# A Strassen step inside the fifth product of the last gate and up stage, with its weight sums kept in DRAM

## The chip, the cores and the metric

The kernel runs on one core of a Trainium2 chip. The metric is device time in microseconds (us) of one execution, lower is better, given as the median of several executions. TensorE (PE) multiplies, VectorE (DVE), ScalarE (ACT) and GpSimd (POOL) work element by element, and SyncE (SP) issues most of the transfers (DMAs).

## The reference

Four residual layers over x of 2048 tokens by 1024 features. Layers 0 and 2 are linear attention (A) with 32 heads, layers 1 and 3 a gated unit (B) of width 3584.

```python
def _A_ref(x, wqkv, wo):                    # phi(t) = (t + 1 if t > 0 else exp(t)) + 1e-6
    q, k, v = split_heads(x @ wqkv)
    kv = einsum("bhsd,bhse->bhde", phi(k), v);  z = phi(k).sum(tokens)
    return merge_heads((phi(q) @ kv) / (phi(q) @ z + 1e-6)) @ wo

def _B_ref(x, W_gate, W_up, W_down):
    gate, up = x @ W_gate, x @ W_up         # (2048 x 1024) @ (1024 x 3584)
    return (relu(gate) * up) @ W_down

x = A_x
x = x + _A_ref(layernorm(x), A_wqkv, A_wo)
x = x + _B_ref(layernorm(x), W_gate, W_up, W_down)
x = x + _A_ref(layernorm(x), A_wqkv, A_wo)
x = x + _B_ref(layernorm(x), W_gate, W_up, W_down)
```

## The kernel before

Each large product is done by the Strassen-Winograd scheme: two matrices of 2x2 blocks are multiplied with seven block products in place of eight, from sums of blocks of the activations and of the weights. In layer B the tokens are worked on in two chunks `c` of 1024, and the columns of gate and up in 14 units `u` of 256 each. `glu` (the function with the matmul line L1154) does one unit: seven products for gate (`g`) and seven for up (`u`), each of four 128x128 weight tiles by 512 token columns, accumulated in one bank of PSUM (the accumulator memory). So a unit is 56 matmuls. The products are numbered as in the text: `five` uses the activation sum s1 (a21 + a22) and is copied by ACT from its bank to a tile `m5` (L1171); `one` goes to bank x, which ACT copies to bank y (L1177); `two` adds to x, `six` adds to y; DVE adds m5 to y, which gives z (L1190); `seven` adds to y and DVE adds the result to m5 (L1203); `three` adds to z, `four` to y. The relus `r` of gate (L1162) and the products `h` (L1165, `put`; L1207 on POOL) close each of the four output blocks. The order of a unit is: five g, one g, five u, one u, two g, six g, two u, six u, 7 g, 3 g, 7 u, 3 u, 4 g, 4 u. A matmul line in the profile names the bank that it writes, so `yg` is product one's bank after six, seven or four, and `vg` is product five.

Where each sum of blocks stands:

- Sums of activations: `sums_x` (L1127 to L1130), four DVE operations for each of four column blocks, ahead of the chunk that uses them.
- Sums of gate and up weights: `make_gu` (L1064 to L1067), made once, in layer 1 chunk 0, by DVE for the unit that comes next, and stored in DRAM as `tg` and `tu` by DMAs on ACT's queue (L1068), one for each weight. All later chunks load the raw weights and these sums again through a ring of buffers (`load_gu`, SP's queue), whose loads are issued five entries ahead of use.
- Sums of down weights: `sums_d`, and for some products of the down stage a second level, `make_dd` and `sums_dd` (L1038), with results in DRAM (`dd`). Those products ("deep", L1319) run seven inner products of 256 columns.

The order of the side work is set by `later`: `later.at(n, f)` runs `f` after n further products (turns), since `mm` in `glu` calls `later.tick()`. `behind(op, f)` issues the operations of f after op on their engine. Instructions of an engine run in the order of issue, and DMAs of SP's queue are issued in SP's order, where one that waits holds back those behind it.

In layer A at the start of layer 2, `phi` (L435, L436, L439) makes the feature map: two ACT operations (relu, exp) into a tile e and one DVE operation. The layer norm of a further group of tokens runs beside it: DVE statistics and `mv` (L195), `ln_root` (ACT, L173 and L174) and the scaled slab (DVE, L180), which a transposing DMA on SP turns to xnT (L410). Query products are the groups qx, qv, qy, qz (L677), with sums by ACT (L670) and DVE (L699, L703).

Of the kernel before, what the change touches and what calls it, by code (L numbers as in the profile page):

```python
# [14 lines left out]
P = 128  # L15
# [77 lines left out]
class _Net:  # L93
    def __init__(self, tc, ctx, x_d, wqkv_d, wo_d, wg_d, wu_d, wd_d, out_d):
# [35 lines left out]
        self.tw = {n: self.spill.tile([P, 8, NW], F16, name=f"t{n}") for n in ("q0", "q1", "k0", "k1")}  # L130
        self.dd = {p: self.spill.tile([P, 7, self.U // 2, NW // 2], F16, name=f"dd{p}") for p in self.DEEP}
        self.later = _Later()
        self.phi_lag = 0
# [50 lines left out]
    def ln_norm(self, layer, t):  # L184
# [14 lines left out]
        def scale(rstd=None if layer == 2 else rstd):  # L199
            if rstd is None:  # L200
                rstd = self.ln_root(mv)
                return lambda: scale(rstd)
# [228 lines left out]
    def phi(self, ps, out):  # L431

        nc = self.nc
        e = self.temp()
        nc.scalar.activation(out=e, in_=ps, func=ACT.Relu, scale=-1.0)  # L435
        nc.scalar.activation(out=e, in_=e, func=ACT.Exp, scale=-1.0, bias=self.eps6[:, 0:1])  # L436

        def join():
            self.last_phi = nc.vector.scalar_tensor_tensor(out=out, in0=ps, scalar=1e-6, in1=e,  # L439
                                                           op0=ALU.max, op1=ALU.add)  # L440

        if self.phi_lag:
            self.later.at(self.phi_lag, join)
        else:
            join()
# [524 lines left out]
    def plan_B(self, l):  # L970
        for c in range(2):
            for u in range(self.U):
                for w in "gu":
                    self.ring.add((l, c, w, u), lambda t, w=w, u=u, first=(l == 1 and c == 0):
                                  self.load_gu(t, w, u, first))
            for p in self.order_d(l, c):
# [64 lines left out]
    def make_dd(self, p, at):  # L1041

        self.later.at(at, lambda: self.load_dd(p))
        for n in range(4):
            self.later.at(at + 18 + 4 * n, lambda n=n: self.behind(self.last_put, lambda n: self.sums_dd(p, n), (n,)))

    def raw_gu(self, t):
        return t[:, 0:4, :].rearrange("p a (b f) -> p (a b) f", f=2 * P)
# [3 lines left out]

    def load_gu(self, t, w, u, first):
        self.nc.sync.dma_start(out=self.raw_gu(t),
                               in_=self.wgu_v[w][:, :, u * 2 * P:(u + 1) * 2 * P])
        if not first:
            self.nc.sync.dma_start(out=t[:, 4:8, :].bitcast(F16), in_=self.tgu[w, u])

# [73 lines left out]
    def ln_chunk(self, l, c, first, step, lag, after):  # L1132
        for j in range(QT):
            for h in range(2):
                self.ln_at(first + (2 * j + h) * step, l, (2 * c + h) * QT + j, lag, after)
            self.later.at(39 + 3 * j, lambda j=j: self.behind(
                self.last_on, lambda j: self.sums_x(l, c, j), (j,)))

    def glu(self, l, c, u, hT):

# [11 lines left out]
        def mm(w, m, ps, start=False):  # L1152
            for k in range(4):
                nc.tensor.matmul(ps, lhsT=W[w][m][:, k, :], rhs=A[m][:, k, :],  # L1154
                                 start=start and k == 0, stop=k == 3, skip_group_check=True)
            later.tick()

        h = hT[u // 2][:, (u % 2) * 4:(u % 2) * 4 + 4, :]
        V, X, Y, Z, R = {}, {}, {}, {}, {}
# [32 lines left out]
        if c == 0 and u == 0:  # L1192
            for f in (one, two, five, six):
                for w in "gu":
                    f(w)
        else:
            for f, f2 in ((five, one), (two, six)):
# [243 lines left out]
    def layer_B(self, l, final):  # L1441
# [6 lines left out]
        for c in range(2):  # L1448
# [3 lines left out]
            for u in range(self.U):  # L1452
# [3 lines left out]
                if first:  # L1456
                    if u + 1 < self.U:
                        self.later.at(4 if u else 9, lambda u=u: behind(self.last_put if u else self.last_z, lambda: [
                            self.make_gu(ring.get((l, c, w, u + 1)), w, u + 1) for w in "gu"]))
                    if u == 3:  # L1460
# [9 lines left out]
                if not final and c == 1:  # L1470
                    if u in (0, 3):
                        self.load_w("qk"[u // 3])
                    if u in (1, 2, 4, 5):
                        for n in range(2):
                            self.later.at(4 + 5 * n, lambda w="qk"[u // 4], n=2 * (u % 3 - 1) + n: behind(
                                self.last_put, lambda: self.sums_w(w, n)))
                if (l, c, u) in ((1, 1, 6), (3, 0, 4)):
                    self.make_dd("T4" if l == 1 else "21", 1)
# [76 lines left out]
```

## Time and profile before

| quantity | value |
|---|---|
| median of three runs | 1448.4 us (1448.38 to 1448.63) |
| the profiled execution | 1447.77 us |
| its span, first to last instruction | 1446.0 us |
| granted TensorE clock | 1.000 |
| busy: PE, DVE, ACT, POOL | 1437.7, 959.7, 613.8, 309.6 us |
| matmuls | 7430 |
| DMA traffic | 304.90 MB |

A time in us from the span's start tells the stage. Layer 1 chunk 0 runs its gate and up products from about 207 to 397; layer 2 starts at 736; layer 3 chunk 0 has gate and up from about 937 to 1113 and the last chunk from about 1194 to 1363, with its down stage up to the end. In a row of the timeline the columns are start, duration, engine, line, operation, output and input; the bracket says how long the engine had been idle and which instruction ended the wait. In a row by stage each engine's busy time is followed by its instruction count in brackets, and the last three columns are granted clock, share of DMA time and GB/s. A row of the chain holds start, length, engine, line and number of instructions. Matmuls overlap, so a group of four appears 1.03 us long in the timeline, though groups start closer together.

### The profile page before, as it was taken

The numbers are of one execution on the slowest core, as the hardware profiler recorded it, in microseconds if no ns is written. First come the engines' busy times: TensorE is split into PE (matmuls) and PEld (weight loads), VectorE is DVE, ScalarE is ACT, GpSimd is POOL, SyncE is SP. The second block draws the span as 40 slices with busy tenths as digits, with TensorE's granted clock in tenths as the row PEclk, the third lists the DMA queues.
The fourth block names the chain that finished last, engine by engine and source line by source line (L and its number), as shares of the span: only waits on it lengthen the run. The fifth ranks groups of instructions, "written<-read, shape, count | busy, mean of one in ns | idle before, by whom it ended". The sixth has DMA issues, their size and how long they took to land.

```text
span 1446.0 us, 20268 instructions
## 1 busy us (share of the span) xinstructions
PE 1437.7 (99%) x7430; PEld 709.2 (49%) x7430; DVE 959.7 (66%) x1799; ACT 613.8 (42%) x1113; POOL 309.6 (21%) x221
## 2 busy tenths in 40 slices
PE   9999999999999999999999999999999999999998
PEld 4444444444455444445654444444444574444457
DVE  7978698677594456549687885764445864444595
ACT  7872564233334334332168726633333433333300
POOL 1453861011100011110031586410111011111002
PEclk9999999999999999999999999999999999999999
DMA  9950787997469999646973119968644799444465
GB/s 287 237 161 8 176 212 204 288 333 255 162 213 288 355 307 307 202 127 220 297 253 88 58 30 266 261 233 269 217 146 130 220 293 323 146 146 146 153 234 181
DMA packets 328836, 304.90 MB, mean 211 GB/s; under 512 B 107456, under 2 KB 291776, under 8 KB 327712
## 3 DMA queue, kind: packets, MB, share of 16 engines
q1 hardware_dynamic: 320688, 282.30, 65.8%
q10 hardware_dynamic: 6560, 17.24, 3.1%
q0 software_dynamic: 1488, 4.07, 0.8%
q8 instruction: 58, 0.95, 0.3%
q14 instruction: 42, 0.34, 0.1%
HBM read 227.28 MB, written 51.64 MB: 193 GB/s over the span
## 4 chain that ended last, share of the span: by engine, by line
PE 92%; DVE 5%; ACT 1%; issue 1%; DMA 1%; SPq 0%; DVEq 0%; ACTq 0%
PE yu L1154 10%; PE yg L1154 10%; PE ps L493 10%; PE dy L1267 8%; PE xu L1154 6%; PE xg L1154 6%; PE dx L1267 6%; PE ps L776 4%; PE zu L1154 3%; PE vg L1154 3%; PE vu L1154 3%; PE zg L1154 3%; PE my L575 3%; PE dyT L1319 2%; PE mv L575 2%; PE mx L575 2%
## 5 line engine op out<-in xcount | busy, mean ns | idle before, releaser
L1154 PEld LDWEIGHTS <-w 128*128 128x128 f16 (+1 forms) x3136 | 306.7, 98 | 372.4 <-issue 3.6
L1207 POOL TENSOR_TENSOR h<-m5u,m5g 128x512 f16<-128x512 f32 x56 | 72.7, 1298 | 721.1 <-DVE m5u L1203 660.0
L493 PE MATMUL ps<-w,xnT 128*128 128x512 bf16 x768 | 169.9, 379 | 0.5 <-ACT xnT L348 0.3
L1190 DVE TENSOR_TENSOR zg<-yg,m5g 128x512 f32<-128x512 f32 x56 | 39.1, 699 | 180.2 <-PE yg L1154 176.1
L493 PEld LDWEIGHTS <-xnT 128*128 128x128 bf16 x768 | 74.4, 98 | 90.0 <-issue 1.6
L1154 PE MATMUL yg<-s,w 128*128 128x512 f16 x448 | 115.0, 379 | 0.3 <-DVE zg L1190 0.3
L1154 PE MATMUL yu<-s,w 128*128 128x512 f16 x448 | 114.9, 379 | 0.1
L1154 PE MATMUL xu<-xnT,w 128*128 128x512 f16 x448 | 115.0, 379 | 0.0
L1154 PE MATMUL xg<-xnT,w 128*128 128x512 f16 x448 | 115.0, 379 | 0.0
L1267 PEld LDWEIGHTS <-h 128*128 128x128 f16 x672 | 65.7, 98 | 78.3
L1162 ACT ACTIVATE m5g<-m5g 128x512 f32<-128x512 f32 x56 | 35.2, 628 | 155.0 <-DVE m5g L1203 155.0
L1319 PEld LDWEIGHTS <-h 128*128 128x128 f16 x966 | 94.5, 98 | 12.3
L436 ACT ACTIVATE e<-e,eps 128x512 f32<-128x512 f32 x128 | 91.0, 720 | 3.2
L723 POOL TENSOR_TENSOR kvc<-pq,kvc 128x1024 f32<-128x1024 bf16 x32 | 78.5, 2454 | 53.1 <-DVE den L728 32.8
L1267 PE MATMUL dx<-w,h 128*128 128x512 bf16 x392 | 85.3, 379 | 0.0
L776 PE MATMUL ps<-T,pqT 128*128 128x512 bf16 x384 | 83.6, 379 | 0.0
L1171 ACT ACTIVATE m5g<-vg 128x512 f32<-128x512 f32 x56 | 33.4, 597 | 108.5 <-PE vg L1154 108.5
L1165 DVE TENSOR_TENSOR h<-yu,r 128x512 f16<-128x512 f32 x56 | 38.7, 691 | 52.8 <-PE yu L1154 52.8
L514 POOL TENSOR_TENSOR kvc<-kvc,slab 128x512 f32<-128x512 f32 x46 | 57.2, 1249 | 76.0 <-DVE slab L439 72.7
L1162 ACT ACTIVATE r<-yg 128x512 f32<-128x512 f32 x56 | 33.4, 597 | 85.2 <-PE yg L1154 85.2
L1203 DVE TENSOR_TENSOR m5u<-yu,m5u 128x512 f32<-128x512 f32 x56 | 38.7, 690 | 46.3 <-PE yu L1154 46.3
L435 ACT ACTIVATE e<-ps 128x512 f32<-128x512 f32 x92 | 54.2, 589 | 28.9 <-PE ps L493 28.8
(234 smaller groups left out, 2385.5 us busy)
## 6 DMA issues: line engine op xcount, KB each, us to landing
w<-in_B_W_gate_dram SPq DMA_DIRECT2D x56, 512.0 KB, 6.1
w<-in_B_W_up_dram SPq DMA_DIRECT2D x56, 512.0 KB, 6.0
w<-tg SPq DMA_DIRECT2D x42, 512.0 KB, 7.3
w<-tu SPq DMA_DIRECT2D x42, 512.0 KB, 6.6
w<-ddT SPq DMA_DIRECT2D x21, 896.0 KB, 6.5
w<-td SPq DMA_DIRECT2D x18, 896.0 KB, 5.0
w<-dd SPq DMA_DIRECT2D x15, 896.0 KB, 5.0
w<-in_B_W_down_dram SPq DMA_DIRECT2D x14, 896.0 KB, 4.9
```

The source lines that it names most:

```text
L435: nc.scalar.activation(out=e, in_=ps, func=ACT.Relu, scale=-1.0)
L436: nc.scalar.activation(out=e, in_=e, func=ACT.Exp, scale=-1.0, bias=self.eps6[:, 0:1])
L493: nc.tensor.matmul(by_row(ps), lhsT=self.xnT[l, l_q][:, kt, j * P:(j + 1) * P], rhs=w[:, kt, :].rearrange("p (b i d) -> p i b d", i=R, d=H ...
L514: nc.gpsimd.tensor_tensor(out=ksum[:, cols], in0=ksum[:, cols], in1=pk, op=ALU.add)
L575: nc.tensor.matmul(banks[j], lhsT=A(i)[:, j * P:(j + 1) * P], rhs=B(i), start=start and i == 0, stop=i == NS - 1, skip_group_check=True)
L723: nc.gpsimd.tensor_tensor(out=prod, in0=pq_of[sc, j], in1=zrow, op=ALU.mult)
L776: nc.tensor.matmul(ps, lhsT=pqT[sc][:, g, j * P:(j + 1) * P], rhs=T[g // 4][:, g % 4, n2 * NW:(n2 + 1) * NW], start=(g == 0), stop=(g == G ...
L1154: nc.tensor.matmul(ps, lhsT=W[w][m][:, k, :], rhs=A[m][:, k, :], start=start and k == 0, stop=k == 3, skip_group_check=True)
L1162: self.last_relu = nc.scalar.activation(out=out, in_=ps, func=ACT.Relu)
L1207: nc.gpsimd.tensor_tensor(out=h[:, 3, :], in0=V["u"], in1=V["g"], op=ALU.mult)
L1267: nc.tensor.matmul(banks[j], lhsT=A(k)[:, j * P:(j + 1) * P], rhs=w[:, i, :], start=start and k == 0, stop=k == self.U - 1, skip_group_che ...
L1319: nc.tensor.matmul(bank[:, j * H:(j + 1) * H], lhsT=A[i // 2][:, i % 2, j * P:(j + 1) * P], rhs=B[m][:, i, :], start=start and i == 0 and ...
```

## The change

In layer 3 chunk 1, product five of gate and up of two neighbouring units (an even u from 2 on, and u + 1) is done together, as a 2x2 block product of its own in seven inner products: `inner_gi` returns them in the order five, one, two, six, seven, three, four, each of four matmuls of 256 columns (weight tiles of gate or up, both halves). They are put in after turns 0, 2, 3, 5, 7, 9 and 11 of the odd unit before the pair; the results go to two SBUF tiles `gi_v`, used in turns by the pairs. The units 2 to 13 leave out their own product five and start one g, one u, two g, six g, two u, six u; the rest is as before. `ready_gi` makes the four inner activation sums once, in unit 0.

The inner weights are 7 sets: three are blocks of the sum for product five that lie in `tg` and `tu` already, and four are differences. `make_gi` runs in layer 3 chunk 0 at units 3, 7 and 9, for two pairs each: it loads the four blocks (8 DMAs), stores three of them as they are, and has DVE make four more (`sums`, eight DVE operations for two pairs) with a store behind each. `load_gi` reads all seven sets of a pair in one DMA of SP at the start of an even unit, into one buffer `gi_w` that lies over two tiles of the residual x. `load_gu` leaves out that quarter of the sums from unit 2 of the last chunk on.

Besides, at layer 2's start `ln_root` is issued behind the last exponential of the feature map (`last_exp`). And in layer 1 chunk 0 `make_gu` for the next unit no longer runs for gate and up at one turn (turn 4, or 9 for unit 0): gate stays there and up follows four turns later.

```diff
--- before.py
+++ after.py
@@ -129,6 +129,7 @@
         self.td = self.spill.tile([P, 4, self.U, NW], F16, name="td")
         self.tw = {n: self.spill.tile([P, 8, NW], F16, name=f"t{n}") for n in ("q0", "q1", "k0", "k1")}
         self.dd = {p: self.spill.tile([P, 7, self.U // 2, NW // 2], F16, name=f"dd{p}") for p in self.DEEP}
+        self.gi = [self.spill.tile([P, 7, 2, 2, P], F16, name=f"gi{p}") for p in range(self.U // 2)]
         self.later = _Later()
         self.phi_lag = 0
 
@@ -198,7 +199,8 @@
 
         def scale(rstd=None if layer == 2 else rstd):
             if rstd is None:
-                rstd = self.ln_root(mv)
+                with self.tc.issue_after(self.last_exp.ins):
+                    rstd = self.ln_root(mv)
                 return lambda: scale(rstd)
             if layer % 2 == 0 and (layer, t // QT) != (2, 0):
                 return self.ln_scale(src, mv, rstd, self.xn_home(layer, t))
@@ -433,7 +435,7 @@
         nc = self.nc
         e = self.temp()
         nc.scalar.activation(out=e, in_=ps, func=ACT.Relu, scale=-1.0)
-        nc.scalar.activation(out=e, in_=e, func=ACT.Exp, scale=-1.0, bias=self.eps6[:, 0:1])
+        self.last_exp = nc.scalar.activation(out=e, in_=e, func=ACT.Exp, scale=-1.0, bias=self.eps6[:, 0:1])
 
         def join():
             self.last_phi = nc.vector.scalar_tensor_tensor(out=out, in0=ps, scalar=1e-6, in1=e,
@@ -971,8 +973,8 @@
         for c in range(2):
             for u in range(self.U):
                 for w in "gu":
-                    self.ring.add((l, c, w, u), lambda t, w=w, u=u, first=(l == 1 and c == 0):
-                                  self.load_gu(t, w, u, first))
+                    self.ring.add((l, c, w, u), lambda t, w=w, u=u, first=(l == 1 and c == 0),
+                                  lo=(l, c) == (3, 1) and u > 1: self.load_gu(t, w, u, first, lo))
             for p in self.order_d(l, c):
                 if self.is_deep(l, c, p):
                     for e in range(4):
@@ -1044,17 +1046,118 @@
         for n in range(4):
             self.later.at(at + 18 + 4 * n, lambda n=n: self.behind(self.last_put, lambda n: self.sums_dd(p, n), (n,)))
 
+    GI_AT = (0, 3, 5), (1, 4, 2, 6)
+
+    def make_gi(self, pairs, at):
+
+        def load():
+            t = self.slot(f"gi{pairs[0]}", [P, 2, 2, 2, 4, P], F16)
+            for i, p in enumerate(pairs):
+                for a in range(2):
+                    for n, w in enumerate("gu"):
+                        self.nc.sync.dma_start(out=t[:, i, n, a, :, :].rearrange("p k f -> p (k f)"),
+                                               in_=self.tgu[w, 2 * p + a][:, 0, :])
+            self.gi_b = [[[t[:, i, :, a, 2 * j:2 * j + 2, :] for a in range(2)] for j in range(2)]
+                         for i in range(2)]
+            self.later.at(4, lambda: [store(i, m, self.gi_b[i][j][a]) for i in range(2)
+                                      for m, j, a in ((0, 0, 0), (3, 1, 0), (5, 1, 1))])
+
+        def store(i, m, b):
+            for n in range(2):
+                self.nc.sync.dma_start(out=self.gi[pairs[i]][:, m, n, :, :], in_=b[:, n, :, :])
+
+        def sums(i, n):
+            (b11, b12), (b21, b22) = self.gi_b[i]
+            out, a, b, m = ((b11, b12, b11, 1), (b12, b22, b12, 4), (b22, b22, b11, 2), (b21, b21, b22, 6))[n]
+            self.nc.vector.tensor_tensor(out=out, in0=a, in1=b, op=ALU.subtract)
+            self.later.at(2, lambda: store(i, m, out))
+
+        self.later.at(at, load)
+        for i in range(2):
+            for n in range(4):
+                self.later.at(at + 12 + 2 * (4 * i + n), lambda i=i, n=n: self.behind(
+                    self.last_put, lambda n: sums(i, n), (n,)))
+
+    def inner_gi(self, p):
+
+        nc, v = self.nc, self.nc.vector
+        H, V, A = NW // 2, self.gi_v[p % 2], self.gi_a
+        B = {m: self.gi_w[:, n] for n, m in enumerate((1, 5, 6, 2, 7, 3, 4))}
+        out = lambda i, a: V[:, a, :, i, :]
+        copy = lambda o, x: nc.scalar.activation(out=o, in_=x, func=ACT.Copy)
+        bank = lambda k: self.kvp.tile([P, 2, H], F32, tag=f"kv{k}", name=f"i{k}")
+        S = {}
+
+        def mm(m, b, start=False):
+            for w in range(2):
+                for k in range(2):
+                    nc.tensor.matmul(b[:, w, :], lhsT=B[m][:, w, k, :], rhs=A[m][:, k, :],
+                                     start=start and w == 0 and k == 0, stop=k == 1, skip_group_check=True)
+
+        def five():
+            z = bank(0)
+            mm(5, z, True)
+            copy(out(1, 1), z)
+
+        def one():
+            S["x"], S["y"] = bank(0), bank(1)
+            mm(1, S["x"], True)
+            copy(S["y"], S["x"])
+
+        def two():
+            mm(2, S["x"])
+            copy(out(0, 0), S["x"])
+
+        def six():
+            mm(6, S["y"])
+            S["z"] = bank(0)
+            v.tensor_tensor(out=S["z"], in0=S["y"], in1=out(1, 1), op=ALU.add)
+
+        def seven():
+            mm(7, S["y"])
+            v.tensor_tensor(out=out(1, 1), in0=S["y"], in1=out(1, 1), op=ALU.add)
+
+        def three():
+            mm(3, S["z"])
+            copy(out(0, 1), S["z"])
+
+        def four():
+            mm(4, S["y"])
+            copy(out(1, 0), S["y"])
+
+        return [five, one, two, six, seven, three, four]
+
+    def ready_gi(self):
+
+        flat = lambda t: self.xall[:, t:t + 2, :].rearrange("p a n -> p (a n)")
+        H = NW // 2
+        self.gi_w = flat(0).bitcast(F16)[:, 0:28 * P].rearrange("p (m w k f) -> p m w k f", m=7, w=2, f=P)
+        self.gi_v = [flat(t).rearrange("p (a w i n) -> p a w i n", a=2, w=2, n=H) for t in (2, 4)]
+        S1, S2, S3, S4 = (self.x[6].bitcast(F16)[:, n * NW:(n + 1) * NW].rearrange("p (k n) -> p k n", n=H)
+                          for n in range(4))
+        s1 = self.xs[3, 1][0]
+        (a11, a12), (a21, a22) = ([s1[:, 2 * j:2 * j + 2, i * H:(i + 1) * H] for j in range(2)] for i in range(2))
+        v = self.nc.vector
+        v.tensor_tensor(out=S1, in0=a21, in1=a22, op=ALU.add)
+        v.tensor_tensor(out=S2, in0=S1, in1=a11, op=ALU.subtract)
+        v.tensor_tensor(out=S3, in0=a11, in1=a21, op=ALU.subtract)
+        v.tensor_tensor(out=S4, in0=a12, in1=S2, op=ALU.subtract)
+        self.gi_a = {1: a11, 2: a12, 3: S4, 4: a22, 5: S1, 6: S2, 7: S3}
+
+    def load_gi(self, p):
+        self.nc.sync.dma_start(out=self.gi_w, in_=self.gi[p])
+
     def raw_gu(self, t):
         return t[:, 0:4, :].rearrange("p a (b f) -> p (a b) f", f=2 * P)
 
     def sums_gu(self, t):
         return t[:, 4:8, :].bitcast(F16).rearrange("p t (k f) -> p t k f", f=P)
 
-    def load_gu(self, t, w, u, first):
+    def load_gu(self, t, w, u, first, lo):
         self.nc.sync.dma_start(out=self.raw_gu(t),
                                in_=self.wgu_v[w][:, :, u * 2 * P:(u + 1) * 2 * P])
         if not first:
-            self.nc.sync.dma_start(out=t[:, 4:8, :].bitcast(F16), in_=self.tgu[w, u])
+            self.nc.sync.dma_start(out=t[:, 4 + lo:8, :].bitcast(F16), in_=self.tgu[w, u][:, lo:4, :])
 
     def make_gu(self, t, w, u):
 
@@ -1136,6 +1239,8 @@
             self.later.at(39 + 3 * j, lambda j=j: self.behind(
                 self.last_on, lambda j: self.sums_x(l, c, j), (j,)))
 
+    INNER_AT = (0, 2, 3, 5, 7, 9, 11)
+
     def glu(self, l, c, u, hT):
 
         nc, later = self.nc, self.later
@@ -1153,8 +1258,13 @@
             for k in range(4):
                 nc.tensor.matmul(ps, lhsT=W[w][m][:, k, :], rhs=A[m][:, k, :],
                                  start=start and k == 0, stop=k == 3, skip_group_check=True)
+            if inner and next(turn) in self.INNER_AT:
+                inner.pop(0)()
             later.tick()
 
+        deep = (l, c) == (3, 1)
+        inner = self.inner_gi(u // 2 + 1) if deep and u % 2 and u + 1 < self.U else []
+        turn = count(0 if u > 1 else -2)
         h = hT[u // 2][:, (u % 2) * 4:(u % 2) * 4 + 4, :]
         V, X, Y, Z, R = {}, {}, {}, {}, {}
 
@@ -1193,6 +1303,13 @@
             for f in (one, two, five, six):
                 for w in "gu":
                     f(w)
+        elif deep and u > 1:
+            for k, w in enumerate("gu"):
+                V[w] = self.gi_v[u // 2 % 2][:, u % 2, k, :, :].rearrange("p i n -> p (i n)")
+            for f in ((one,), (two, six)):
+                for w in "gu":
+                    for g in f:
+                        g(w)
         else:
             for f, f2 in ((five, one), (two, six)):
                 for w in "gu":
@@ -1455,8 +1572,10 @@
                 ring.load_to(ring.index((l, c, "g", u)) + 5)
                 if first:
                     if u + 1 < self.U:
-                        self.later.at(4 if u else 9, lambda u=u: behind(self.last_put if u else self.last_z, lambda: [
-                            self.make_gu(ring.get((l, c, w, u + 1)), w, u + 1) for w in "gu"]))
+                        for n, w in enumerate("gu"):
+                            self.later.at((4 if u else 9) + 4 * n, lambda u=u, w=w: behind(
+                                self.last_put if u else self.last_z,
+                                lambda: self.make_gu(ring.get((l, c, w, u + 1)), w, u + 1)))
                     if u == 3:
                         for d in (self.U - 4, self.U - 2):
                             wd[d] = self.load_d(d)
@@ -1474,6 +1593,12 @@
                         for n in range(2):
                             self.later.at(4 + 5 * n, lambda w="qk"[u // 4], n=2 * (u % 3 - 1) + n: behind(
                                 self.last_put, lambda: self.sums_w(w, n)))
+                if (l, c) == (3, 0) and u in (3, 7, 9):
+                    self.make_gi({3: (1, 2), 7: (3, 4), 9: (5, 6)}[u], 1)
+                if (l, c, u) == (3, 1, 0):
+                    self.later.at(4, lambda: behind(self.last_put, self.ready_gi))
+                if (l, c) == (3, 1) and u % 2 == 0 and u + 2 < self.U:
+                    self.later.at(5 if u == 0 else 1, lambda u=u: self.load_gi(u // 2 + 1))
                 if (l, c, u) in ((1, 1, 6), (3, 0, 4)):
                     self.make_dd("T4" if l == 1 else "21", 1)
                 if c == 0 and u == 1:
```

## The prediction

> **What bounds the kernel now.** I read the page's engine table and end chain first, then the same counts by stage, then the end chain inside the stage that is changed, then the rows around each TensorE stall.
>
> ```profile
> PE 1437.7 (99%) x7430; PEld 709.2 (49%) x7430; DVE 959.7 (66%) x1799; ACT 613.8 (42%) x1113; POOL 309.6 (21%) x221
> PE 92%; DVE 5%; ACT 1%; issue 1%; DMA 1%; SPq 0%; DVEq 0%; ACTq 0%
> 207.20:397.00 189.80, 189.24 (x875) 85.32 (x873) 138.53 (x249) 71.42 (x123) 20.67 (x15) 1.00 0.81 248
> 736.00:822.00 86.00, 84.37 (x390) 37.86 (x389) 71.02 (x125) 67.14 (x120) 30.18 (x26) 1.00 0.37 104
> 1196.00:1363.00 167.00, 167.00 (x775) 75.73 (x774) 67.32 (x97) 64.22 (x111) 17.78 (x14) 1.00 0.54 175
> ```
>
> TensorE (PE) is the bound. The last row, gate and up of the last chunk, is full: PE 167.00 of 167 us at granted clock 1.00, VectorE (DVE) 40%, ScalarE (ACT) 38%. There only fewer or shorter matmuls can save. In the first two rows (layer 1 chunk 0; start of layer 2) PE misses 0.56 and 1.63 us of busy time (stalls counted from matmul starts: 1.40 and 2.36), so there edits elsewhere can pay.
>
> ```profile
> 1210.20 0.86 PE yg L1154 x4
> 1211.06 0.86 PE xu L1154 x4
> 1211.92 0.86 PE yu L1154 x4
> 1387.18 1.53 PE dxT L1319 x14
> 1388.71 1.53 PE dzT L1319 x14
> ```
>
> A group of four 512-column matmuls takes 0.863 us of the chain (starts 1210.20, 1211.06, 1211.92): 0.2158 each. The deep products of the down stage already run 256 columns: 1.53 us per 14, 0.1092 each.
>
> **The changed product.** Units 2 to 13 of layer 3 chunk 1, six pairs. Removed per pair: product five of two units, two weights, 16 x 0.2158 = 3.453 us. Added: seven inner products of 4 at 256 columns, 28 x 0.1092 = 3.058. Saved 0.395 a pair, **2.37 us**, all on the path.
>
> The rule that speaks against it is in the Trainium skill, "TensorE: Matmul & The Clock Gate", Back-to-back issue gap: in streams of weight load and matmul it gives about 131 ns a matmul at 512 columns and 81 at 128. On a straight line 256 columns is an estimated 98, so 28 x 98 = 2.74 replaces 16 x 131 = 2.10: a loss of 0.65 a pair, 3.9 us in all. This trace shows 215.8 and 109.2 in just such streams; I take the trace, 2.37.
>
> **Waits in the odd units.** The inner products of the next pair are put between the outer ones of the odd unit: after one g, two g, six g, six u, three g, three u, four u. Outer group to ACT start is 1.06 us (931.57 to 932.63 below).
>
> ```profile
> 931.57 1.03 PE L1154 MATMUL xg<-xnT,w 128*128 128x512 f16 x4
> 932.63 0.58 ACT L1177 ACTIVATE yg<-xg 128x512 f32<-128x512 f32 x1 [7.61 <-PE xg L1154]
> 933.30 1.03 PE L1154 MATMUL xg<-xnT,w 128*128 128x512 f16 x4
> ```
>
> From the unit's start: one g 0, inner five 0.86, one u 1.30, two g 2.16, inner one 3.03, six g 3.46, inner two 4.33. The relu r0 of two g starts at 2.16 + 1.06 = 3.22; inner one's copy stands behind it, 3.76 to 4.34; inner two adds to the copied bank and may start 0.08 later, 4.42. Late by 0.1 to 0.15, six times: **+0.6** (bounds 0, if the copy starts sooner, and 2). In even units one g, one u, two g follow with nothing between; the rows above have that spacing with no stall. Other copies and the two DVE sums have a group or more of slack. Per pair ACT loses four copies and gains five, DVE gains two sums: both near 40% busy, no cost.
>
> **Its data.** Four DVE sums of 128x512 f16 (0.42 each, rows of L1127) at about 1195 to 1199 lie in idle DVE. The weights: six reads of 896 KB into one buffer, freed by the previous odd unit's last inner product, needed after an even unit and one group: 12 x 0.863 + 0.863 = 11.2 us.
>
> ```profile
> w<-dd SPq DMA_DIRECT2D x15, 896.0 KB, 5.0
> ```
>
> The same size lands in 5.0: about 6 us slack. The first read waits on SP's queue for DVE to finish the residual tiles it overwrites (about 1171), ahead of two transposes that feed the activation sums; those end at 1186.5, wanted at 1193.5: 7 us slack. The smaller t loads cut 3 MB.
>
> The sums of these weights are made in layer 3 chunk 0 (units 3, 7, 9): 24 reads of 128 KB, 84 stores of 64 KB in 512 B runs, 24 DVE sums of 0.42. SP's queue takes all of them ahead of later ring loads; the ring lands about 20 us ahead there (up of unit 10: 1045.3, used about 1066), at 0.62 DMA share. "Perfetto Trace Analysis", DMA Optimizations, says transfers under 2 KB carry a significant overhead each; at 64 KB the stores are the part I trust least. PE loses only 0.19 us in that stage, so there is nothing to gain; I charge 0, bounds 0 and 1. The DVE sums fit the 0.75 us between the z sum and seven u.
>
> **Layer 2's start.** The square root of the layer norm is put behind the last feature-map Exp.
>
> ```profile
> 743.44 0.29 ACT L173 ACTIVATE rstd<-mv,eps 128x1 f32<-128x1 f32 x1 [2.09 <-DVE mv L195]
> 743.88 0.58 ACT L435 ACTIVATE e<-ps 128x512 f32<-128x512 f32 x1
> 751.31 0.69 DVE L699 TENSOR_TENSOR qz<-qy,qm 128x512 f32<-128x512 f32 x1
> 752.06 1.02 PE L677 MATMUL qy<-w,s 128*128 128x512 f16 x4 [1.03 <-DVE qz L699]
> ```
>
> ACT stood 2.09 us for a mean/variance with ready exponentials behind it (that at 743.88 could go at 741.73). The lateness runs through ACT and DVE to qz, done at 752.00; PE loses 1.19 there and 0.28 before it. With rstd behind them the same rows, replayed with their own durations, put qz's end at 749.7; it must be before 752.00 - 1.19 - 0.28 = 750.5. **Gain 1.4** (bounds 0 and 1.5). Late next: the normalised slabs, by 10 to 15 us, whose transposes are still in time for the sums at about 792.5.
>
> **Layer 1's sums.** The next unit's weight sums go from one block after put 0 to gate at turn 4, up at turn 8, four turns (3.5 us) later.
>
> ```profile
> 301.95 1.29 DVE L1064 TENSOR_TENSOR w<-w 128x1024 f16<-128x1024 bf16 x2
> 303.15 0.75 DVE L1066 TENSOR_TENSOR w<-w 128x512 f16<-128x512 bf16 x2
> 303.82 0.75 DVE L1067 TENSOR_TENSOR w<-w 128x512 f16<-128x512 bf16 x2
> 306.10 0.69 DVE L1190 TENSOR_TENSOR zg<-yg,m5g 128x512 f32<-128x512 f32 x1
> 306.84 1.02 PE L1154 MATMUL yg<-s,w 128*128 128x512 f16 x4 [0.31 <-DVE zg L1190]
> ```
>
> The block is 2.8 us of DVE; with the deep-weight sums behind it zg came late and PE lost 0.47. Split, this stall and that at 225.5 (0.12) go. But half of it, about 1.3 us, now stands ahead of zu, or of a unit's deep sum. The up sums' store moves with them: one DMA issue of 0.4 us on ACT's queue, three turns (2.6 us) after the sums, where the next unit's copy of vg stands behind it; the sums are done by then, and it is read back only a chunk later, so it costs 0. Replaying the order of DVE by hand, unit 1 (also with a 1.15 us activation sum) loses about 0.84, the unit with a deep sum ahead of zu 0.60, one more 0.14. Net **+0.9** (bounds -0.8, the old stalls and part of the next, and +1.5): the same work, in another place.
>
> **The sum.** -2.37 + 0.6 - 1.4 + 0.9 = -2.3 us. The profiled execution took 1447.77 (span 1446.0, 1.77 around it); it becomes 1445.5, span 1443.7. The median shown is 1448.4, 0.63 above: forecast **1446.1**. About 0.2% (2.9 us) is what a measurement of this kernel can tell from no change, so by this sum the gain is just under it.
>
> **The rivals.**
> A. As summed, or with one term at its poor bound (layer 2 gains nothing, or the inner wait is 0.3): -0.5 to -2.9. For it: every term has a row. Chance 0.53; at 1446.1.
> B. The waits do not come: PE finds the copy done at inner two, layer 1 loses half of its old 0.59 and gains no stall: -2.37 - 1.4 - 0.3 = -4.1, 1444.3. For it: three of four terms are hidden if DVE's order is a microsecond kinder than my replay. Against it: the tight spot is computed from steady rows. Chance 0.37.
> C. Slower: the inner weights come late. One buffer, so each read waits for the last inner product, and 7 KB per partition lies behind whatever SP holds. A read landing 11.2 us after its release costs nothing; each us beyond costs five pairs 1 us each. The 2.3 are gone at 11.7 us (0.46 late), slower by 0.2% from 12.3 (1.04 late); at 13 the result is -2.3 + 5 x 1.8 = +6.7, 1455. For it: the stage moves 175 GB/s at 0.54 share. Against it: 5.0 us for that size. Chance 0.10, with the skill's matmul rate (+3.9 in place of -2.37) in it.
> That the products do not shrink is out: the changed kernel's instruction order has 96 fewer 512-column matmuls and 168 more of 256 columns.
>
> **Numbers.** Low 1444.0 is B with all 0.59 of layer 1 gone (-4.4). High 1449.1 is A with layer 2's gain gone and layer 1 and the stores at their poor bounds (-2.3 + 1.4 + 0.6 + 1 = +0.7); about 1 in 10 lies above it, in C, and less below. Faster by over 0.2%: 0.37; within: 0.53; slower: 0.10.
>
> **What would show it.** Right: PE in the last gate and up stage falls from 169.2 us (14 units x 56 x 0.2158) to about 167.4, an inner group of four takes 0.437, a small PE wait on ACT at inner two; no stall at qy (752); layer 1's stalls move to zu groups. Wrong: a PE wait on DMA at the first inner product (C), inner matmuls above 0.11 us, or stalls in layer 3 chunk 0 behind the stores.

## The result and the profile after

The changed kernel takes 1445.29 us (median of 15 runs, 1445.14 to 1446.05) against 1448.61 (15 runs, 1447.95 to 1449.86): ratio 0.9977, 95% interval 0.9969 to 0.9985, a gain of 3.3 us. The forecast was 1446.1 and "within 0.2%" as the likeliest outcome; the time lies in the range and 0.8 below the forecast. The gain is just past 2.9 us, the size that the prediction took as the least that can be told from no change, and the interval (2.2 to 4.5 us) lies on both sides of it. By the profiled executions alone the gain is smaller: 1447.77 to 1445.22, -2.55 us, where the sum said -2.3.

The page's engine table, and the stages of before as windows of after (columns as before; the end of the changed stage is 2.5 us earlier):

```profile
PE 1436.3 (100%) x7502; PEld 716.7 (50%) x7502; DVE 980.0 (68%) x1839; ACT 615.7 (43%) x1119; POOL 308.7 (21%) x221
207.20:397.00 189.80, 189.02 (x873) 85.18 (x872) 138.94 (x248) 71.79 (x123) 20.00 (x15) 1.00 0.80 248
736.00:822.00 86.00, 85.33 (x394) 38.37 (x393) 72.21 (x127) 69.44 (x129) 31.23 (x27) 1.00 0.39 112
937.00:1113.00 176.00, 176.00 (x816) 79.73 (x815) 97.00 (x157) 63.61 (x109) 17.78 (x14) 1.00 0.78 245
1193.20:1360.50 167.30, 167.30 (x858) 83.69 (x856) 77.18 (x114) 67.61 (x118) 18.65 (x16) 1.00 0.60 189
```

72 matmuls more, yet 1.4 us less PE time. Layer 2's start has about 1 us more PE work in the same window; layer 1's first chunk is no better. Layer 3 chunk 0 (fourth row), where the inner weights are made, stays full although its DMA share rose to 0.78 (0.62 before) and VectorE's work by 10 us. Counted from the starts of the matmuls, the stalls of TensorE by stage are:

| stage | before | after |
|---|---|---|
| layer 1 chunk 0, gate and up | 1.40 | 1.71 |
| layer 2's start | 2.36 | 1.24 |
| layer 3 chunk 0, gate and up | 0.19 | 0.19 |
| last chunk, gate and up | 0.00 | 0.49 |
| start of the kernel (0 to 104) | 2.88 | 3.04 |

The other stages agree within 0.01. So: -2.37 of matmuls, +0.49, -1.12, +0.31, +0.16 (start) is -2.53, and the two executions differ by 2.55. The start of the kernel is not touched by the change; over all thirteen traces its stalls range from 2.88 to 3.65.

The chain of after at both ends of the last gate and up stage, and all matmuls of the inner products by their line:

```profile
1191.64 1.53 PE dyT L1436 x14
1193.17 0.86 PE vg L1259 x4
1359.58 0.86 PE yu L1259 x4
1360.45 1.73 PE dx L1384 x8
L1094 PE MATMUL i<-x x96: 272/273/273, 1207.7 to 1337.2; 128*128 128x256 f16 x96
L1094 PE MATMUL i<-s,x x72: 269/272/273, 1209.8 to 1339.4; 128*128 128x256 f16 x72
```

The stage runs from 1193.17 to 1360.45, 167.28 us; before it was 1193.79 to 1363.01, 169.22. The forecast had 167.4. (The 272 ns of a matmul holds its tail; starts are 109 ns apart.)

### The profile page after: what moved, and what is told of

Same layout as the page of the kernel before. It is cut to its first block, busy times and chain, and to the rows that moved or that the text cites. A ratio compares the mean times of both kernels' runs of the same rounds, so it can differ in the third digit from the quotient of the medians.

```text
span 1443.4 us, 20611 instructions
## 1 busy us (share of the span) xinstructions
PE 1436.3 (100%) x7502; PEld 716.7 (50%) x7502; DVE 980.0 (68%) x1839; ACT 615.7 (43%) x1119; POOL 308.7 (21%) x221
## 4 chain that ended last, share of the span: by engine, by line
PE 94%; DVE 4%; ACT 1%; issue 1%; DVEq 0%; ACTq 0%
PE ps L495 11%; PE yu L1259 10%; PE yg L1259 10%; PE dy L1384 8%; PE xg L1259 6%; PE xu L1259 6%; PE dx L1384 6%; PE ps L778 4%; PE zu L1259 3%; PE zg L1259 3%; PE my L577 3%; PE vu L1259 3%; PE vg L1259 3%; PE dyT L1436 2%; PE mv L577 2%; PE mx L577 2%
## 5 line engine op out<-in xcount | busy, mean ns | idle before, releaser
L1259 PEld LDWEIGHTS <-w 128*128 128x128 f16 (+1 forms) x3040 | 297.3, 98 | 352.6 <-issue 3.9
L1324 POOL TENSOR_TENSOR h<-m5u,m5g 128x512 f16<-128x512 f32 x44 | 56.6, 1286 | 594.7 <-DVE m5u L1320 555.5
L1300 DVE TENSOR_TENSOR zg<-yg,m5g 128x512 f32<-128x512 f32 x44 | 30.7, 699 | 130.7 <-PE yg L1259 126.8
L1272 ACT ACTIVATE r<-zg 128x512 f32<-128x512 f32 x56 | 32.8, 586 | 84.3 <-PE zg L1259 84.3
L1281 ACT ACTIVATE m5g<-vg 128x512 f32<-128x512 f32 x44 | 26.3, 597 | 95.2 <-PE vg L1259 95.2
L737 POOL TENSOR_TENSOR pq<-pq,den 128x1024 bf16<-128x1024 bf16 x32 | 61.2, 1911 | 6.8 <-DVE den L732 5.0
```

The source lines that it names most:

```text
L737: nc.gpsimd.tensor_tensor(out=heads(pq), in0=heads(pq), in1=den[:, :].unsqueeze(2).to_broadcast([P, D // HD, HD]), op=ALU.mult)
L1272: self.last_relu = nc.scalar.activation(out=out, in_=ps, func=ACT.Relu)
L1324: nc.gpsimd.tensor_tensor(out=h[:, 3, :], in0=V["u"], in1=V["g"], op=ALU.mult)
```

## The experiments

### Each part alone

The three parts were taken apart: the inner products alone, the root alone, the split of the weight sums alone, and all but the split. The edits, against the kernel before or after:

```diff
 # root alone, on the kernel before
-                rstd = self.ln_root(mv)
+                with self.tc.issue_after(self.last_exp.ins):
+                    rstd = self.ln_root(mv)
 # without the split, on the changed kernel (the split alone is the reverse, on before;
 # the products alone is this and the reverse of the root, on the changed kernel)
-                        for n, w in enumerate("gu"):
-                            self.later.at((4 if u else 9) + 4 * n, lambda u=u, w=w: behind(
-                                self.last_put if u else self.last_z,
-                                lambda: self.make_gu(ring.get((l, c, w, u + 1)), w, u + 1)))
+                        self.later.at(4 if u else 9, lambda u=u: behind(self.last_put if u else self.last_z, lambda: [
+                            self.make_gu(ring.get((l, c, w, u + 1)), w, u + 1) for w in "gu"]))
```

> The fifth products by inner products with their data, but the root at layer 2's start and the weight sums of layer 1 as before. My theory (the three parts add): span of the profile 1446.0 - 2.37 + 0.49 = 1444.1, and TensorE stalls 1.40 in layer 1 chunk 0 and 2.36 at layer 2's start as before, 0.49 in the last gate and up stage. Rival (the root is what pays, the inner products bring nothing once their waits and the transfers in layer 3 chunk 0 are counted): span within 0.4 of 1446.0.

> Before, with only the root put behind the last exponential. My theory: the stalls of 1.19 at qy and 0.28 at qx go and 0.35 comes at about 778, so the span is 1446.0 - 1.1 = 1444.9. Rival (the gain depends on what the other parts shift): no change beyond 0.3.

> Before, with only the sums of the next unit's weights one weight at a time. My theory: the stalls at 306.84 and 225.45 go, new ones of 0.66, 0.20 and 0.16 come, layer 1 chunk 0 has 1.7 in place of 1.4: span 1446.3. Rival (its own theory, that shorter blocks of VectorE help): span 1445.4 or less.

> The changed kernel with the weight sums of layer 1 as before. My theory: stalls of layer 1 chunk 0 back at 1.4, span 1443.4 - 0.3 = 1443.1, time 0.3 below the changed kernel. Rival: the split hides a longer wait elsewhere, and the span is 1443.8 or more.

| kernel | span | median (runs) | ratio, interval | layer 1 | layer 2 | last stage |
|---|---|---|---|---|---|---|
| products alone | 1444.3 | 1446.64 (21) | 0.9987, 0.9980 to 0.9993 | 1.40 | 2.35 | 0.49 |
| root alone | 1445.4 | 1447.26 (21) | 0.9992, 0.9986 to 0.9999 | 1.40 | 1.23 | 0.00 |
| split alone | 1446.4 | 1448.30 (13) | 1.0002, 0.9993 to 1.0010 | 1.69 | 2.35 | 0.00 |
| all but the split | 1443.6 | 1445.40 (12) | 0.9978, 0.9970 to 0.9986 | 1.88 | 1.23 | 0.49 |

(The kernel before: 1448.55, median of 56 runs on the same chip; the last three columns are TensorE stalls in us.) The stalls of each stage belong to one part each (but for layer 1 in the fourth row, see below), and the parts add: against 1448.55 the medians give -1.9, -1.3 and -0.25, together -3.5, for 3.3 measured. The first expectation held to 0.2 us; the second missed by 0.5, of which 0.45 is a stall at 479.2, ahead of layer 1's second chunk, that no other of these four executions has; the third held (the split alone brings nothing that can be told from zero); the fourth did not: without the split the span is 1443.6, not 1443.1, and layer 1 has more stalls than before, not 1.40. The reason is below.

Layer 2 behaves as the replay said. The timeline of after at the place shown of before:

```profile
743.93 0.60 ACT L437 ACTIVATE e<-ps 128x512 f32<-128x512 f32 x1 [0.37 <-DVE stats L164]
745.19 0.28 ACT L174 ACTIVATE rstd<-mv,eps 128x1 f32<-128x1 f32 x1
749.37 0.69 DVE L701 TENSOR_TENSOR qz<-qy,qm 128x512 f32<-128x512 f32 x1
751.07 1.03 PE L679 MATMUL qy<-w,s 128*128 128x512 f16 x4
776.28 0.81 DVE L181 TENSOR_SCALAR slab<-x,mv,rstd 128x1024 bf16<-128x1024 f32 x1
777.01 0.69 DVE L441 SCALAR_TENSOR_TENSOR pq<-qy,e 128x512 bf16<-128x512 f32 x1
777.75 1.46 PE L495 MATMUL ps<-w,xnT 128*128 128x512 bf16 x6 [0.18 <-DVE pq L441]
```

The rstd no longer stands ahead of ready exponentials; qz ends at 750.06, a whole microsecond before qy starts at 751.07, with no wait in brackets. What came late in its place is in the last three rows: a scaled slab now stands ahead of a pq (before, the last slab was done at 762.3), and TensorE loses 0.35 us there by the starts of its matmuls. The root alone has the same 1.23 us in this stage, so it is the root that brings both. That makes -1.12 in place of -1.4.

### Why the split alone is worth nothing in one execution and something in another

In the kernel without the split the timeline of layer 1 chunk 0 has rows that the kernel before also has, only shorter. First two of before, then those of all but the split:

```profile
314.11 0.69 DVE L1064 TENSOR_TENSOR w<-w 128x1024 f16<-128x1024 bf16 x1 [0.53 <-DMA w<-in_B_W_up_dram]
326.74 0.69 DVE L1064 TENSOR_TENSOR w<-w 128x1024 f16<-128x1024 bf16 x1 [0.86 <-DMA w<-in_B_W_up_dram]
```

```profile
315.08 0.69 DVE L1167 TENSOR_TENSOR w<-w 128x1024 f16<-128x1024 bf16 x1 [1.29 <-DMA w<-in_B_W_up_dram]
316.81 0.33 ACTq L1171 DMA_DIRECT2D tg<-w  x1
317.19 0.58 ACT L1287 ACTIVATE yu<-xu 128x512 f32<-128x512 f32 x1 [1.57 <-DVE w L1170]
317.82 1.02 PE L1259 MATMUL xu<-xnT,w 128*128 128x512 f16 x4
```

VectorE's sums wait for the raw up weights to land; gate's store, issued on ACT's queue, waits for the sums; behind it stands the copy yu, and behind that TensorE's two u. A wait of 0.53 is absorbed, and 1.29 gives a stall of 0.19; one unit on, 0.86 is absorbed and 1.17 gives 0.28. The instructions of the two kernels stand in the same order in this stage. The products alone and the root alone, which also lack the split, wait 0.43 and 0.33 at the first place and 0.53 at the second, without a stall: one of four executions has it. Neither of the two traces with the split (split alone, after) has a wait of VectorE for this transfer in that stage. So the split does something that my sum left out: it gives the up weights four turns, 3.5 us, more. To test it, an eighth of the up weights of units 9 and 10 is read a second time, behind the first reading, with and without the split:

```diff
         self.nc.sync.dma_start(out=self.raw_gu(t),
                                in_=self.wgu_v[w][:, :, u * 2 * P:(u + 1) * 2 * P])
+        if first and w == "u" and u in (9, 10):
+            self.nc.sync.dma_start(out=self.raw_gu(t)[:, 7:8, :],
+                                   in_=self.wgu_v[w][:, 7:8, u * 2 * P:(u + 1) * 2 * P])
```

> Before, with the raw up weights of units 9 and 10 in layer 1 chunk 0 made to land later: an eighth of them is read a second time behind the first reading, some 2.5 to 3 us more. My theory (the split does not save VectorE time, it gives the up weights 3.5 us more to land, and without it a late landing goes through VectorE's sums and the store on ACT's queue to the copies that TensorE waits for): stalls of 1.5 to 2.5 us at each of about 317 and 330, layer 1 chunk 0 at 4.5 to 6.5 in place of 1.4. Rival (the split is only about the length of the block of VectorE): no stall beyond 0.5 more, since the sums have the rest of the unit.

> The same late up weights, with the sums split by weight as in the change. My theory: the later turn covers the lateness, layer 1 chunk 0 stays at 1.7 to 2.2. Rival: as much stall as the kernel with the late weights and without the split.

Without the split (timeline):

```profile
330.63 0.69 DVE L1067 TENSOR_TENSOR w<-w 128x1024 f16<-128x1024 bf16 x1 [3.91 <-DMA w<-in_B_W_up_dram]
332.73 0.58 ACT L1180 ACTIVATE yu<-xu 128x512 f32<-128x512 f32 x1 [4.40 <-DVE w L1070]
333.37 1.02 PE L1157 MATMUL xu<-xnT,w 128*128 128x512 f16 x4 [2.86 <-ACT yu L1180]
350.09 0.69 DVE L1067 TENSOR_TENSOR w<-w 128x1024 f16<-128x1024 bf16 x1 [3.85 <-DMA w<-in_B_W_up_dram]
351.63 0.69 DVE L1193 TENSOR_TENSOR zu<-yu,m5u 128x512 f32<-128x512 f32 x1
352.38 1.86 PE L1157 MATMUL yu<-s,w 128*128 128x512 f16 x4 [3.06 <-DVE zu L1193]
```

The same execution by stage, right behind the second of these waits (the third number from the end is the granted clock):

```profile
352.30:356.00 3.70, 3.62 (x10) 1.33 (x10) 1.73 (x5) 1.11 (x2) 0.88 (x1) 0.56 0.84 284
```

With the split (timeline):

```profile
345.32 0.69 DVE L1067 TENSOR_TENSOR w<-w 128x1024 f16<-128x1024 bf16 x1 [1.31 <-DMA w<-in_B_W_up_dram]
345.93 0.69 DVE L1193 TENSOR_TENSOR zu<-yu,m5u 128x512 f32<-128x512 f32 x1
346.68 1.02 PE L1157 MATMUL yu<-s,w 128*128 128x512 f16 x4 [0.98 <-DVE zu L1193]
```

The spans are 1454.9 and 1447.8 (one execution each), the stage's stalls 9.25 and 2.83 us. The same late transfer costs 7.9 us on the one kernel (1.40 to 9.25) and 1.1 on the other (1.69 to 2.83). Both numbers are above what I expected, but the order is clear: a late transfer costs much more without the split. Its way to TensorE is not the same at both places. The first stall (3.02 by the starts of the matmuls, at 333.37) comes through ACT's queue, as my theory said. The second (3.23, at 352.38) does not: in that unit of the program as built, the up sums stand between zg and zu on VectorE, and zu comes late; the stall with the split takes this way too. And 1.5 of the 7.9 us are no wait: behind the second stall TensorE ran at a granted clock of 0.56. Behind the first it stayed at 1.00 (333.30 to 337.00).

That the late transfer is also what parts the profile's gain (-2.55) from that of the medians (-3.3) is not shown, and by the medians the split itself is worth nothing that can be told: 1445.29 with it and 1445.40 without, 1448.30 and 1448.55 on the kernel before. The spread does not settle it: 1448.15 to 1450.13 with the split alone, 1447.84 to 1449.95 without. What is sure is that before's profiled execution, 1447.77, lies 0.84 under its median, and the changed kernel's, 1445.22, only 0.07 under its own.

### The wait at inner two

```diff
-    INNER_AT = (0, 2, 3, 5, 7, 9, 11)
+    INNER_AT = (0, 2, 4, 5, 7, 9, 11)
```

> The changed kernel with inner product two one turn later (turns 0, 2, 4, 5, 7, 9, 11). My theory (inner two waits for ACT's copy of its bank, which stands behind a relu): the 0.04 to 0.10 before each inner two goes, 0.3 in all, and the 0.03 at two g of the even units stays: 0.2 in the last gate and up stage, span 1443.1. Rival (a fixed cost of changing from 512 to 256 columns): the 0.04 stays wherever inner two stands, span 1443.4.

First the timeline of the changed kernel, then that of this one:

```profile
1233.94 0.60 ACT L1272 ACTIVATE r<-xg 128x512 f32<-128x512 f32 x1 [0.31 <-PE xg L1259]
1234.12 1.03 PE L1259 MATMUL yg<-s,w 128*128 128x512 f16 x4
1234.43 0.59 ACT L1087 ACTIVATE i<-i 128x512 f32<-128x512 f32 x1
1235.08 0.60 PE L1094 MATMUL i<-s,x 128*128 128x256 f16 x4
```

```profile
1234.13 1.03 PE L1259 MATMUL yg<-s,w 128*128 128x512 f16 x4
1234.99 1.03 PE L1259 MATMUL xu<-xnT,w 128*128 128x512 f16 x4
1235.85 0.60 PE L1094 MATMUL i<-s,x 128*128 128x256 f16 x4
```

Between yg and inner two lie 0.96 us in the first, 0.863 without a wait: the copy behind the relu ends at 1235.02. This is the pair with the longest wait, because the relu starts 1.12 us after its group; in the first pair it starts after 1.06, and the wait there and in the four other pairs is 0.04. With inner two one turn later the next group follows at 0.86. The stage's stalls fall from 0.49 to 0.20, as my theory said; what is left is 0.03 at two g of each unit without inner products. Median 1445.01 (10 runs, 1444.79 to 1445.8), ratio 0.9974, interval 0.9964 to 0.9983: the lowest median of the kernels here. It is 0.3 us below the changed kernel's, as the trace would have it, but the two intervals overlap, so the times alone do not show it.

### The price of late inner weights

`load_gi` issues its transfer three times in a row, each behind the landing of the one before.

```diff
         self.nc.sync.dma_start(out=self.gi_w, in_=self.gi[p])
+        self.nc.sync.dma_start(out=self.gi_w, in_=self.gi[p])
+        self.nc.sync.dma_start(out=self.gi_w, in_=self.gi[p])
```

> The changed kernel with the inner weights of each pair read three times, each after the landing of the one before. The price that the prediction gave for late inner weights: one reading lands 4.6 us after the release and 11.2 are to be had, so three in a row land at about 14 to 15, late by 3 to 4, five pairs: 15 to 20 us more, span 1458 to 1463, waits at inner five on DMA. Rival (SP's queue, held by the third reading, delays the ring's loads as well): more than 25 us, waits at the outer products too. Or nothing, if there is more slack than 11.2.

One reading lands 4.7 us after its issue in the median of the six (the first, ahead of the stage, takes 7.7):

```profile
DMA to landing us min/median/max: 4.6/4.7/7.7
```

With three, the chain of that kernel at the stage's start, one of its inner fives (timeline), and the stage's start as a row by stage:

```profile
1189.48 8.21 DMA w<-tg
1197.69 0.05 issue
1197.74 1.89 PE vg L1261 x4
1242.12 0.61 PE L1094 MATMUL i<-x 128*128 128x256 f16 x4 [0.43 <-DMA x<-gi]
1197.70:1202.40 4.70, 4.66 (x12) 1.57 (x13) 0.00 (x0) 1.18 (x2) 0.00 (x0) 0.53 1.10 364
```

The span is 1456.9, +13.5. The mechanism is there, but not at my price: 4.6 us is lost once, at the first outer product (vg), because the readings hold back the ring's loads on SP's queue, which is the rival's mechanism. Another 2.2 goes right behind it, where TensorE runs at a granted clock of 0.53, and 0.3 at an outer product at 1239.59. The pairs lose 0.6 to 1.8 at inner five, 6.2 in five places, in place of 3 to 4 each: in the program built for this kernel inner five stands three outer groups later (behind one u, two g, six g and the first matmul of two u of the odd unit, where the changed kernel has it right behind one g), so about 2.8 us of lateness is covered. The order of the instructions is set when the kernel is built, and it changed with the loads.

### Three tries at the rest of layer 1

The larger stalls that the split brings lie at 236.5 (0.66) and 297.6 (0.20), where up sums stand ahead of zu. The up sums were put six turns after gate's in place of four, and, in two more kernels, left with gate's in two units alone; all three with inner two at turn 4.

```diff
-                            self.later.at((4 if u else 9) + 4 * n, ...
+                            self.later.at((4 if u else 9) + 6 * n, ...                                # six later
+                            self.later.at((4 if u else 9) + (0 if u in (2, 7) else 4) * n, ...        # all but two
+                            self.later.at((4 if u else 9) + (0 if u in (1, 6) else 4) * n, ...        # all but 1 and 6
```

> The changed kernel with inner product two at turn 4, and the up sums of layer 1 chunk 0 six turns behind gate's in place of four, so that in the unit with the activation sums (zu at 235.8) zu stands ahead of them on VectorE. My theory (the split's cost is only the up sums' first operation ahead of zu): the stall of 0.65 at 236.5 goes, layer 1 chunk 0 falls from 1.7 to about 1.1, span 1442.6, median about 1444.4. Rival (VectorE is full in that unit, so the lateness moves to the next operation that TensorE waits for): stalls of the same sum behind zu, at yg or at the next unit's vg, span 1443.2.

> The changed kernel with inner product two at turn 4, and with the split left out in units 2 and 7 of layer 1 chunk 0 alone, where up sums stand ahead of a late zu (stalls 0.65 and 0.20). My theory (each place has its own balance, the split pays where up weights land late and costs where VectorE is full ahead of zu): the two stalls go, layer 1 chunk 0 at 0.9, span 1442.4, median about 1444.3. Rival (the block in one piece delays zg there as much as the halves delay zu): no less than 1.6, span 1443.1 or more.

> The same as the kernel with the split left out in two units, now for units 1 and 6, in which the stalls of 0.65 and 0.20 ahead of zu lie (units 2 and 7 left them where they were). My theory: both go, layer 1 chunk 0 at about 0.9 to 1.0, span 1442.5, median about 1444.3. Rival (the block in one piece delays zg as much as the halves delay zu): layer 1 chunk 0 at 1.6 or more, span 1443.1 or more.

All three missed. Six turns later: 1445.69 (17 runs), span 1443.7; zu comes ahead of the up sums, yet 0.48 stays at 235.8 and a stall of 1.15 comes at 308.1 before yg; at 297 it helps, with 0.03 left and 0.14 one product later. All but units 2 and 7: the wrong units, both stalls stay; 1445.13 (11 runs). All but 1 and 6: 1445.24 (15 runs), stalls of 0.52 at 236.1 and 0.20 at 297.5, layer 1 at 1.79. Only unit 1 was the right one. The stall at 297.5 lies in unit 5 (five u of units 5 and 6 starts at 289.5 and 301.8), where the trace still has the up sum on its own ahead of zu (296.13 and 296.73), so this kernel does not test that place. The timeline of the last shows what stands ahead of zu at 236, and below it the same stretch of before:

```profile
230.64 1.22 DVE L548 TENSOR_TENSOR sT<-T 128x2048 f16<-128x2048 bf16 x1
231.89 1.22 DVE L548 TENSOR_TENSOR T<-T,T 128x2048 f16<-128x2048 bf16 x1
233.03 0.69 DVE L1300 TENSOR_TENSOR zg<-yg,m5g 128x512 f32<-128x512 f32 x1
233.63 1.22 DVE L548 TENSOR_TENSOR sT<-T,sT 128x2048 f16<-128x2048 bf16 x1
234.76 0.68 DVE L1275 TENSOR_TENSOR h<-xu,r 128x512 f16<-128x512 f32 x1
235.37 0.69 DVE L1300 TENSOR_TENSOR zu<-yu,m5u 128x512 f32<-128x512 f32 x1
```

```profile
230.60 1.22 DVE L546 TENSOR_TENSOR sT<-T 128x2048 f16<-128x2048 bf16 x1
232.19 0.70 DVE L1190 TENSOR_TENSOR zg<-yg,m5g 128x512 f32<-128x512 f32 x1 [0.38 <-PE yg L1154]
232.80 1.22 DVE L546 TENSOR_TENSOR T<-T,T 128x2048 f16<-128x2048 bf16 x1
234.54 0.69 DVE L1190 TENSOR_TENSOR zu<-yu,m5u 128x512 f32<-128x512 f32 x1
235.73 1.22 DVE L546 TENSOR_TENSOR sT<-T,sT 128x2048 f16<-128x2048 bf16 x1
```

The rows of 1.22 us, which the expectations call activation sums, are sums of the blocks of T, a factor of the output product of layer 0 (`sums_T`). In the last kernel VectorE has no gap, and three of them stand ahead of zu. Before has only two there, the third is behind zu, and VectorE even waits 0.38 us for TensorE: no stall. In the changed kernel, and with the up sums six turns later, all four stand ahead of zu. So what these traces point to at this place is, for the most part, the sums of T, which stand earlier in the order as built than before: with the up sums behind zu, 0.48 of 0.66 stays. No run moved the sums of T alone, and why the build has them earlier stays open.

## Why the prediction was right, and where it was off

- **The changed product.** Right: matmuls of the inner products start 109 ns apart, so 0.395 a pair stands, and the products alone bring 1.7 us of span and 1.9 of median. The spacing that the prediction took from the Trainium skill ("TensorE: Matmul & The Clock Gate", Back-to-back issue gap: about 131 ns a matmul at 512 columns) would have made it a loss of an estimated 3.9; the 215.8 and 109 ns of these traces decide against it here.
- **Waits in the odd units.** The place and the cause were right; the size was 0.04 to 0.10 a pair (0.28 in all), not 0.1 to 0.15. The replay itself gave 0.09 (4.42 less 4.33) and was rounded up; and copies start 0.50 us behind a relu and matmuls 0.05 to 0.06 behind the copy, where it had 0.54 and 0.08. The 0.03 at two g of each of the seven units without inner products, which I had called free, makes up most of the difference: 0.49 for 0.6. There the copy of one g starts 1.12 us after its group (1220.27 to 1221.39), not 1.06.
- **Its data.** Zero, as charged: layer 3 chunk 0 has stalls of 0.19 before and after, with the small stores in it, and the inner weights land 4.65 us after issue at the second pair (1220.46 to 1225.11), 6.4 us ahead of inner five at 1231.52.
- **Layer 2's start.** The replay put qz's end at 749.7 on before's clock; it is 750.06 on a clock that is 0.48 later at that point (qx at 743.73 for 743.25). The 1.47 of stalls went as said. The slabs' lateness, which the prediction named but followed only to the transposes, costs 0.35 at a pq; it is also larger than said, 19 us for the last slab (761.53 to 780.74) in place of 10 to 15.
- **Layer 1's sums.** This is the term that was mis-sized: +0.9 predicted, +0.31 measured. All three places were right (236.5, 297.6 and 335.2), with 0.84, 0.60 and 0.14 predicted for 0.66, 0.20 and 0.16 measured; and a stall of 0.18 at 248.7 went that the sum had not counted. At the first place, the largest, the cause was only in part the one named: four sums of T stand ahead of zu where before had two, and the prediction counted one. And the step behind it was incomplete: it treated the split as a rearrangement of VectorE's work and did not ask which of the operands might be late. The trace of before had the answer in four waits of 0.2 to 0.9 us for the up weights.
- **The sum.** -2.3 for -2.5 by stages. That it comes so close is in part luck: layer 1 turned out 0.6 better than charged, layer 2 0.3 worse, and the start of the kernel 0.16 worse. The transfer from the profiled execution to the median added the same 0.63 to both kernels; before's 15 runs lie 0.84 above its profile and after's only 0.07, which carries the median over the 2.9 us that the forecast placed just out of reach. Why before's median lies so far above its profile stays open.
- **The rivals.** A's band was too wide by its own terms (one of them at its poor bound gives -0.9 to -2.6, not -0.5 to -2.9). B's -4.1 was too much, and the waits that it left out came; C did not happen: the readings come 6 us early, where C had them late, and its price is partly another's, as the threefold reading shows.

## What to carry to other kernels

In a stage that TensorE fills, count its time from the starts of its own matmuls at each width before trusting a general spacing; then a change of block products is worth what the count says, and the rest is a handful of waits of a tenth of a microsecond that can be placed one by one. When work is moved on an element-wise engine, ask of each operand when it lands and what stands behind it on every queue that its stores go through: a wait that is absorbed in the one profiled execution may not be in the next. And where an engine is full for several microseconds, look at the whole order that the build gives it: moving one kind of work away let another move in ahead of the operation that TensorE waits for.

## What I had not expected of the hardware

Four kernels with the same order of instructions in that stage waited 0.33, 0.43, 0.53 and 1.29 us for the same transfer (up weights at about 314), enough to make a TensorE stall come and go. A single long wait cost more than itself: behind 4.6 and 3.2 us the granted clock was 0.53 and 0.56 in the rows of 4.7 and 3.7 us, and TensorE lost another 2.2 and 1.5. In layer 3 chunk 0 the DMA share rose from 0.62 to 0.78 and the rate from 197 to 245 GB/s with 512-byte runs among the stores, without one stall more.
